# Convolution beside a feed-forward product: the second term of stage 1 summed in PSUM, the spectra multiplied in wider operations, and three row tiles taking turns

## The chip, the cores and the metric

The kernel runs on one core of a Trainium2 chip. The core has a matrix engine (TensorE, PE in the profile), VectorE (DVE), ScalarE (ACT), GpSimd (POOL) and SyncE (SP); each runs its own list of instructions in order, and semaphores tie the lists together. SBUF holds tiles of 128 partitions, and PSUM has eight banks of 128 x 512 float32 for the results of PE. DMA queues move data to and from DRAM. The metric is the device time of one execution in microseconds.

## What is computed

Two branches work on the layer-normalized input and are added to the input itself (2048 rows, 1024 channels, a hidden width of 3584):

```python
xn = layernorm(x)                                        # x = A_q, 1 x 2048 x 1024
k_shift = sum over 4 taps of shifted k * shift_k         # causal, per channel
kv = k_shift * v
y = irfft(rfft(kv, 4096) * rfft(ssm_k, 4096))[:2048]     # long causal convolution per channel
y = y + kv * ssm_D
conv = xn * y
ffn = silu(xn @ w1) @ w2                                 # 1024 -> 3584 -> 1024
return x + conv + ffn
```

Everything is float32. For the products in PE each operand is split into a float16 part `hi` and a float16 remainder `lo`, and each float32 product becomes three matmuls: hi by hi, hi by lo, lo by hi.

## The kernel before

*How the order of the work comes about.* No engine's list is written out by hand. Each part of the work is a Python generator (a stream) that yields operations: `T` for PE, `V` for DVE, `A` for ACT, `L` for a DMA issued by SP, `G` for a DMA issued by POOL that adds to what stands in DRAM (`accum_op=ADD`). `Order.run` takes, again and again, the operation that could start earliest by a model of engine times, less the bias of its stream; that puts it at the end of its engine's list. A stream can also yield a condition (a `Token`, or a free buffer) and is passed over until it holds. `Ring` is a set of named buffers; a tile that is taken from it is free again when its token has been set often enough. The bank rings of PSUM are `ff` (4 banks), `ps` (2), `px` (1) and `py` (1). Of the SBUF rings these matter here: `wo` (13 operand tiles, used for W1's factors and then for h), `v` (2), `hf` (3), `xg` (2), `yt` (2), `zh` and `zl` (2 each), `hi` and `lo` (2 each), `tmp` (1).

*The feed-forward branch* (`feed_forward`, from line 841). The first product runs per unit of hidden columns as seven block products P1 to P7 on sums and differences of blocks (`steps`, matmuls of 128 x 512 at lines 761 to 763); `evacuate` copies intermediate sums out of PSUM on ACT (into `v`, `w`) and adds them back on DVE (`hf<-ff,w`, `hf<-ff,v`); `block` applies SiLU, splits and writes h to DRAM. When that product is done, the second one runs: for each half `h` of 512 output columns and each of 16 row tiles `t`, one bank of `ff` collects 7 chunks `c` of 4 x 3 matmuls (lines 868 to 870), 84 in all, 2688 for the whole. `load_h` brings h's chunks on SP's queue in the order in which PE reads them. W2's chunks (`w2c[h, c]`) are split by `norms_w2` into places that the first product has left; the first row tile of a half is the first reader of each chunk. `result` scales a finished tile on ACT into a `v` buffer, and POOL adds it to the output. `copies` first writes x to the output (SP, line 918), one block of 128 rows after each half unit of the first product; no accumulating write may start before all sixteen copies are in the list (`flag["copied"]`).

*The convolution* (`convolution`). It goes over 8 groups `g` of 128 channels, beside the matrix products of the other branch, once the first part of the first product is over. For each group:
- `gate` makes `kv` and its energy; `norm` turns energies into powers of two as scales (a small matmul with ones, a DVE chain);
- `signal_parts`: for each of four `t` (in the order 1, 3, 0, 2) four transposes into `px` (line 1100) and splits into `hi`, `lo`;
- `stage1` (lines 1108 to 1134): a transform of length 128 as matmuls with the constants `cfw`. For each `t` and each half `c` (real, imaginary) two terms `i`, each of three matmuls of 128 x 512 into a bank of its own, from `ps` or, when the first product is over and more than one bank of `ff` is free (`spare`), from `ff`;
- `to_spec` (lines 1140 to 1150): with p0 and p1 the two banks, `total` = p0 (ACT copy), `diff` = total - p1, `total` = total + p1 (both DVE, reading PSUM);
- `forward`: the steps between the eight sub-transforms, on DVE;
- `product` (lines 1189 to 1227): the complex product of the two spectra, four pairs at a time, with `tmp`, a `zh` and a `zl` buffer as scratch; ACT squares the result for its energy, writing the squares to a `yt` buffer;
- `inverse`, `result_parts` (splits into `zh`, `zl`), `stage1_inv` (12 matmuls of 128 x 256 per `t` into `py`, lines 1331 to 1333), and `gated`: DVE multiplies `py` by the normalized rows `xg` into a `yt` buffer, and POOL adds that to the output in two writes (line 252), after which the buffer is free.

`stage1` of group g+1 starts when `product` of group g is over, since both use the spectrum `spec`. Four `gated` tiles per group and two `yt` buffers mean that the third and the fourth wait for the writes of the first and the second.

*Helpers whose lines appear in the profile:* line 248 is `L` (SP DMA), 252 `G` (POOL DMA), 255 `v_tt` (DVE, two tensors), 258 `v_stt` (DVE, scalar and two tensors), 266 `a_act` (ACT). Many parts share these lines, so they are told apart by the names of their tiles.

Of the kernel before, what the change touches and what calls it, by code (L numbers as in the profile page):

```python
# [12 lines left out]
BF16 = mybir.dt.bfloat16  # L13
F16 = mybir.dt.float16
# [198 lines left out]
def h3_ffn_kernel(ctx, tc, x, kp, vs, fs, shift, dskip, w1, w2, cfwd, cinv, out):  # L213
# [627 lines left out]
    def feed_forward():  # L841
# [12 lines left out]
        for h in range(2):  # L854
            for t in range(NT):
                yield ff.ready
                po, tok = ff.tile([P, W])
                final = (h, t) == (1, NT - 1)
                if final:
                    add(last_result(h, t, po, tok), EB)  # L860
                for c in range(NF // 4):
                    yield flag["h", h, t, c]
                    hx, htok = flag["h", h, t, c].what
                    yield flag["w2", h, c]
                    wc, wtok = w2c[h, c]
                    for jj in range(4):
                        def mm(jj=jj, j=4 * c + jj):
                            nc.tensor.matmul(po, hx[:, jj, 0, :], wc[:, jj, 0, :], start=(j == 0), stop=False)  # L868
                            nc.tensor.matmul(po, hx[:, jj, 0, :], wc[:, jj, 1, :], start=False, stop=False)  # L869
                            nc.tensor.matmul(po, hx[:, jj, 1, :], wc[:, jj, 0, :], start=False, stop=(j == NF - 1))  # L870
                        yield T(mm, po, [hx[:, jj], wc[:, jj]], 3 * 0.2185)
                    htok.set()
                    if t == NT - 1:
                        wtok.set()
                if final:
                    flag["last"].set()
                else:
                    add(result(h, t, po, tok), EB)
# [24 lines left out]
    def load_h():  # L903
        yield flag["factors"]
        for h in range(2):
            for t in range(NT):
                for c in range(NF // 4):
                    yield wo.ready
                    flag["h", h, t, c].what = o, _ = wo.tile([P, 4, 2, P], F16)
                    yield L(o, hs[t // 4][t % 4][:, 4 * c:4 * c + 4])  # L910
                    flag["h", h, t, c].set()
# [69 lines left out]
    def pair(a, b):  # L981
# [3 lines left out]
                       ap=[list(a.ap[0]), [b.offset - a.offset, 2]] + [list(d) for d in a.ap[1:]])  # L985

    TO = (1, 3, 0, 2)

    def convolution(floor):
# [118 lines left out]
        def stage1():  # L1108

            for g in range(NG):  # L1110
# [4 lines left out]
                for t in TO:  # L1115
                    yield flag["part", g, t]
                    (hi, htok), (lo, ltok) = part.pop((g, t))
                    for c in range(2):
# [343 lines left out]
```

## Time and profile before

| what | value |
| --- | --- |
| three runs | 1296.42, 1298.86, 1302.47 us |
| median | 1298.86 us |
| profiled execution, its own time | 1299.35 us |
| span of the profile in it | 1297.6 us |
| mean granted PE clock | 0.993 of full speed |

The page of the profile has one line per engine of how busy it is in 40 slices of the span, each slice 32.4 us long. A digit is the busy share in tenths (9 is 90% or more); PEclk is the granted clock in the same way:

```profile
PE   7899999999999998999999999999999999999998
DVE  8999997889999759999899899899899989989920
ACT  6867987887766856768523412512562252241120
POOL 0000000000000011001100200210110021011021
PEclk8999999999999998999999999999999999999999
```

PE is below nine tenths in the first two slices (layernorm and the first factors come before there is much to multiply), in the sixteenth (from 487 to 519 us) and in the last. In the rows below, a row of a timeline has the start in us, the duration in us, the engine, the line, the operation, out<-in tiles, sizes and types, and in brackets how long the engine stood before it and what ended that. A row of groups has the same for all instructions of one kind: count, busy us in sum, mean ns of one, then the idle time just before them and what ended most of it.

### The profile page before, as it was taken

To read this page: it belongs to the slowest core of one execution; us is meant where nothing else is said; L and a number is where in the kernel's file an instruction comes from. 1 tells how busy PE (TensorE), PEld (TensorE's weight loads), DVE (VectorE), ACT (ScalarE), POOL (GpSimd) and SP (SyncE) were. 2 spreads that over 40 slices of the span, in tenths; PEclk is the share of its full clock that TensorE was granted. 3 is DMA by queue.
4 is the path that set the end of the run, shared out by engine and by line. 5 is a ranking of instruction groups with operands and counts; after the bars stand their busy time and mean duration, and the time that the engine had idled before them with its cause. 6 is when DMAs were issued, how large, how long until landed. Compare 5 with 4: busy or idle time off the path is not lost.

```text
span 1297.6 us, 17976 instructions
## 1 busy us (share of the span) xinstructions
PE 1268.9 (98%) x6242; PEld 618.4 (48%) x6242; DVE 1145.9 (88%) x1758; ACT 691.9 (53%) x1238; POOL 98.4 (8%) x101
## 2 busy tenths in 40 slices
PE   7899999999999998999999999999999999999998
PEld 6444544444444543445444544544544454454453
DVE  8999997889999759999899899899899989989920
ACT  6867987887766856768523412512562252241120
POOL 0000000000000011001100200210110021011021
PEclk8999999999999998999999999999999999999999
DMA  9456899789998879869954664674596367456462
GB/s 324 163 163 211 291 318 311 255 263 348 323 324 284 273 214 285 262 207 296 294 168 100 148 186 136 151 191 129 137 290 190 97 156 190 111 112 133 114 138 33
DMA packets 207003, 269.93 MB, mean 208 GB/s; under 512 B 15416, under 2 KB 121920, under 8 KB 204480
## 3 DMA queue, kind: packets, MB, share of 16 engines
q1 hardware_dynamic: 185040, 252.26, 60.7%
q0 software_dynamic: 21872, 16.52, 10.3%
q8 instruction: 49, 0.80, 0.2%
q14 instruction: 42, 0.34, 0.1%
HBM read 193.22 MB, written 83.89 MB: 214 GB/s over the span
## 4 chain that ended last, share of the span: by engine, by line
PE 71%; DVE 17%; DMA 6%; issue 4%; ACT 2%; POOL 0%; SPq 0%; DVEq 0%; ACTq 0%; POOLq 0%
PE ff L763 12%; PE ff L761 12%; PE ff L762 12%; PE ff L869 9%; PE ff L870 9%; PE ff L868 9%; DVE spec L255 5%; DVE tmp L255 3%; DVE acc L258 2%; DMA out<-yt 2%; DMA kin<-in_kp 1%; DVE x L258 1%; PE ps L1127 1%; PE ps L1129 1%; PE ps L1128 1%
## 5 line engine op out<-in xcount | busy, mean ns | idle before, releaser
L869 PE MATMUL ff<-x,wo 128*128 128x512 f16 x896 | 340.7, 380 | 1.3 <-DVE x L258 1.3
L868 PE MATMUL ff<-x,wo 128*128 128x512 f16 x896 | 340.5, 380 | 0.8 <-ACT x L266 0.8
L870 PE MATMUL ff<-x,wo 128*128 128x512 f16 x896 | 340.5, 380 | 0.0
L761 PE MATMUL ff<-x,wo 128*128 128x512 f16 (+1 forms) x808 | 305.1, 378 | 5.7 <-ACT v L266 4.2
L762 PE MATMUL ff<-x,wo 128*128 128x512 f16 (+1 forms) x808 | 305.0, 377 | 2.1 <-DVE x L258 2.1
L763 PE MATMUL ff<-x,wo 128*128 128x512 f16 (+1 forms) x808 | 304.8, 377 | 2.1 <-DVE wo L258 2.1
L255 DVE TENSOR_TENSOR spec<-spec 128x512 f32<-128x512 f32 (+2 forms) x192 | 219.4, 1175 | 1.3
L870 PEld LDWEIGHTS <-wo 128*128 128x128 f16 x896 | 87.7, 98 | 107.7 <-issue 2.4
L868 PEld LDWEIGHTS <-wo 128*128 128x128 f16 x896 | 88.6, 99 | 101.1 <-issue 0.8
L869 PEld LDWEIGHTS <-wo 128*128 128x128 f16 x896 | 87.7, 98 | 102.2 <-issue 1.7
L252 POOL DMA_DIRECT2D out<-yt x64 | 70.5, 1102 | 810.2 <-DMA w2n<-in_w 430.9
L763 PEld LDWEIGHTS <-wo 128*128 128x128 f16 x808 | 79.4, 98 | 99.5 <-DVE wo L258 4.7
L762 PEld LDWEIGHTS <-wo 128*128 128x128 f16 x808 | 79.4, 98 | 92.4 <-issue 6.4
L761 PEld LDWEIGHTS <-wo 128*128 128x128 f16 x808 | 80.6, 100 | 88.5 <-ACT wo L266 2.1
L255 DVE TENSOR_TENSOR tmp<-spec 128x512 f32<-128x512 f32 (+1 forms) x112 | 100.3, 915 | 0.2
L258 DVE SCALAR_TENSOR_TENSOR ht<-hf,wsc,ht 128x512 f16<-128x512 f32 x112 | 83.4, 746 | 17.9 <-ACT ht L266 17.6
L266 ACT ACTIVATE ht<-hf,wsc 128x512 f16<-128x512 f32 x112 | 80.9, 722 | 3.6
L258 DVE SCALAR_TENSOR_TENSOR acc<-kin,taps,acc 128x512 f32<-128x512 f32 x96 | 71.7, 747 | 2.1 <-ACT acc L266 1.9
L266 ACT ACTIVATE xg<-xg,nmr,rstd 128x128 f32<-128x128 f32 x128 | 54.8, 482 | 34.9 <-DMA xg<-in_x 33.5
L266 ACT ACTIVATE zh<-spec,csc 128x1024 f16<-128x1024 f32 x32 | 36.1, 1142 | 66.4 <-DVE spec L258 49.1
L266 ACT ACTIVATE yt<-spec 128x1024 bf16<-128x1024 f32 x32 | 33.7, 1053 | 67.6 <-DVE spec L255 67.4
L266 ACT ACTIVATE v<-ff,invc 128x512 f32<-128x512 f32 x31 | 21.2, 683 | 89.5 <-PE ff L870 89.5
(151 smaller groups left out, 1756.2 us busy)
## 6 DMA issues: line engine op xcount, KB each, us to landing
wo<-hs SPq DMA_DIRECT2D x224, 256.0 KB, 3.0
hs<-ht SPq DMA_DIRECT2D x112, 256.0 KB, 4.6
ws<-wo SPq DMA_DIRECT2D x84, 256.0 KB, 3.6
wo<-ws SPq DMA_DIRECT2D x84, 256.0 KB, 3.7
w2n<-in_w SPq DMA_DIRECT2D x80, 256.0 KB, 4.7
raw<-in_w SPq DMA_DIRECT2D x28, 512.0 KB, 5.5
kin<-in_kp SPq DMA_DIRECT2D x32, 448.0 KB, 3.7
xt<-in_x SPq DMA_DIRECT2D x16, 512.0 KB, 7.2
```

Of the source, the lines that this page charges most:

```text
L252: return Op("POOL", 1.1, 4.0, lambda: nc.gpsimd.dma_start(o, i, accum_op=ADD), [i], [o], m, n)
L255: return V(lambda: nc.vector.tensor_tensor(o, a, b, op=op), o, [a, b], **k)
L258: return V(lambda: nc.vector.scalar_tensor_tensor(o, a, s, b, op0=op0, op1=op1), o, [a, b] + ([] if isinstance(s, float) else [s]), **k)
L266: nc.scalar.activation(o, i, func, scale=scale, **kw)
L761: nc.tensor.matmul(o, w[:, 0, k], xf[:, :, k, 0], start=first and k == 0, stop=False, **kw)
L762: nc.tensor.matmul(o, w[:, 0, k], xf[:, :, k, 1], start=False, stop=False, **kw)
L763: nc.tensor.matmul(o, w[:, 1, k], xf[:, :, k, 0], start=False, stop=last and k == KH - 1, **kw)
L868: nc.tensor.matmul(po, hx[:, jj, 0, :], wc[:, jj, 0, :], start=(j == 0), stop=False)
L869: nc.tensor.matmul(po, hx[:, jj, 0, :], wc[:, jj, 1, :], start=False, stop=False)
L870: nc.tensor.matmul(po, hx[:, jj, 1, :], wc[:, jj, 0, :], start=False, stop=(j == NF - 1))
L1127: nc.tensor.matmul(ps, cf[:, 0, cs], hi[:, i], start=True, stop=False)
L1128: nc.tensor.matmul(ps, cf[:, 0, cs], lo[:, i], start=False, stop=False)
```

## The change

Four things are edited.

1. *Stage 1.* The two terms of a pair now use one bank. The first term's three matmuls write it (for both `c`), ACT copies it to `diff` (times 2), and then the second term's matmuls accumulate upon it in the same bank; they wait for the copy (`seen`). ACT then copies the sum to `total`, and DVE takes one difference: 2 p0 - (p0 + p1) = p0 - p1. The loops over `i` and `c` change places, so that the first terms of both `c` come ahead of the second ones.
2. *Product.* The products of the spectra are taken in operations of 2048, 1024 and 512 elements, through access patterns written out by `steps_of` and `run`, partly in place in the second spectrum; `zh` and `zl` are no longer used for it, nor a `yt` buffer for the squares, which go into a part of the spectrum that is no longer needed. With that `transforms` no longer waits for `more`, the rings that come late.
3. *Second matrix product.* In the first half, the row tiles 0, 1 and 2 take turns: chunk `c` is multiplied for all three before chunk `c + 1`, with three banks open at once (`TOGETHER`). All other row tiles go one by one, as before. `load_h` follows the same order.
4. *What follows from it for the lists.* The scheduler lays all lists out anew with these costs and conditions. The number of matmuls is the same.

```diff
         flag["gemm1"].set()
         for h in range(2):
-            for t in range(NT):
-                yield ff.ready
-                po, tok = ff.tile([P, W])
-                final = (h, t) == (1, NT - 1)
-                if final:
-                    add(last_result(h, t, po, tok), EB)
+            for ts in TOGETHER[h]:
+                pos = {}
                 for c in range(NF // 4):
-                    yield flag["h", h, t, c]
-                    hx, htok = flag["h", h, t, c].what
-                    yield flag["w2", h, c]
-                    wc, wtok = w2c[h, c]
-                    for jj in range(4):
-                        def mm(jj=jj, j=4 * c + jj):
-                            nc.tensor.matmul(po, hx[:, jj, 0, :], wc[:, jj, 0, :], start=(j == 0), stop=False)
-                            nc.tensor.matmul(po, hx[:, jj, 0, :], wc[:, jj, 1, :], start=False, stop=False)
-                            nc.tensor.matmul(po, hx[:, jj, 1, :], wc[:, jj, 0, :], start=False, stop=(j == NF - 1))
-                        yield T(mm, po, [hx[:, jj], wc[:, jj]], 3 * 0.2185)
-                    htok.set()
-                    if t == NT - 1:
-                        wtok.set()
-                if final:
-                    flag["last"].set()
-                else:
-                    add(result(h, t, po, tok), EB)
+                    for t in ts:
+                        final = (h, t) == (1, NT - 1)
+                        if c == 0:
+                            yield ff.ready
+                            pos[t] = ff.tile([P, W])
+                            if final:
+                                add(last_result(h, t, *pos[t]), EB)
+                        yield flag["h", h, t, c]
+                        hx, htok = flag["h", h, t, c].what
+                        yield flag["w2", h, c]
+                        wc, wtok = w2c[h, c]
+                        for jj in range(4):
+                            def mm(jj=jj, j=4 * c + jj, po=pos[t][0]):
+                                nc.tensor.matmul(po, hx[:, jj, 0, :], wc[:, jj, 0, :], start=(j == 0), stop=False)
+                                nc.tensor.matmul(po, hx[:, jj, 0, :], wc[:, jj, 1, :], start=False, stop=False)
+                                nc.tensor.matmul(po, hx[:, jj, 1, :], wc[:, jj, 0, :], start=False, stop=(j == NF - 1))
+                            yield T(mm, pos[t][0], [hx[:, jj], wc[:, jj]], 3 * 0.2185)
+                        htok.set()
+                        if t == NT - 1:
+                            wtok.set()
+                        if c == NF // 4 - 1:
+                            if final:
+                                flag["last"].set()
+                            else:
+                                add(result(h, t, *pos[t]), EB)
+    TOGETHER = ([range(3)] + [(t,) for t in range(3, NT)],
+                [(t,) for t in range(NT)])
...
-            for t in range(NT):
-                for c in range(NF // 4):
-                    yield wo.ready
-                    flag["h", h, t, c].what = o, _ = wo.tile([P, 4, 2, P], F16)
-                    yield L(o, hs[t // 4][t % 4][:, 4 * c:4 * c + 4])
-                    flag["h", h, t, c].set()
+            for c, t in [(c, t) for ts in TOGETHER[h] for c in range(NF // 4) for t in ts]:
+                yield wo.ready
+                flag["h", h, t, c].what = o, _ = wo.tile([P, 4, 2, P], F16)
+                yield L(o, hs[t // 4][t % 4][:, 4 * c:4 * c + 4])
+                flag["h", h, t, c].set()
...
+    def steps_of(a, start, *dims):
+        return run(a, start, 1, *dims)
+    def run(a, start, n, *dims):
+        return bass.AP(tensor=a.tensor, offset=a.offset + start,
+                       ap=[list(a.ap[0])] + [list(d) for d in dims] + [[1, n * P]])
...
                 for t in TO:
                     yield flag["part", g, t]
                     (hi, htok), (lo, ltok) = part.pop((g, t))
-                    for c in range(2):
-                        cs = slice(c * P, (c + 1) * P)
-                        two = []
-                        for i in range(2):
-                            yield lambda: ps_r.ready() or spare()
-                            ps, tok = (ps_r if ps_r.ready() else ff).tile([P, 2, 2 * P])
-                            cf = cfw[:, t + 4 * i]
+                    two = []
+                    for i in range(2):
+                        for c in range(2):
+                            if i == 0:
+                                yield lambda: ps_r.ready() or spare()
+                                ps, tok = (ps_r if ps_r.ready() else ff).tile([P, 2, 2 * P])
+                                two.append((ps, Token(), Token(), Token()))
+                                diff = (tmp[:, :, t // 2] if t % 2 else sp[:, :, 5 + t])[:, :, c]
+                                add(to_spec(g, t, sp[:, :, t, c, :], diff, *two[c], tok), CB)
+                            ps, seen, made = two[c][:3]
+                            if i == 1:
+                                yield seen
 
                             def mm():
-                                nc.tensor.matmul(ps, cf[:, 0, cs], hi[:, i], start=True, stop=False)
-                                nc.tensor.matmul(ps, cf[:, 0, cs], lo[:, i], start=False, stop=False)
-                                nc.tensor.matmul(ps, cf[:, 1, cs], hi[:, i], start=False, stop=True)
+                                cf = cfw[:, t + 4 * i, :, c * P:(c + 1) * P]
+                                kw = dict(skip_group_check=i == 1)
+                                nc.tensor.matmul(ps, cf[:, 0], hi[:, i], start=i == 0, stop=False, **kw)
+                                nc.tensor.matmul(ps, cf[:, 0], lo[:, i], start=False, stop=False, **kw)
+                                nc.tensor.matmul(ps, cf[:, 1], hi[:, i], start=False, stop=True, **kw)
                             yield T(mm, ps, [hi[:, i], lo[:, i]], 0.65, m=2.0)
-                            two += [ps, tok]
-                        diff = (tmp[:, :, t // 2] if t % 2 else sp[:, :, 5 + t])[:, :, c]
-                        add(to_spec(g, t, sp[:, :, t, c, :], diff, *two), CB)
+                            (made if i else two[c][3]).set()
                     htok.set()
                     ltok.set()
 
         def spare():
             return flag["gemm1"]() and len(ff.free()) > 1
 
-        def to_spec(g, t, total, diff, p0, tok0, p1, tok1):
+        def to_spec(g, t, total, diff, ps, seen, made, half, tok):
+            yield half
             if g > 0:
                 yield flag["taken", g - 1, t]
                 if t % 2 == 0:
                     yield flag["taken", g - 1, t + 1]
-            yield a_act(total, p0, AF.Copy)
-            tok0.set()
-            yield v_tt(diff, total, p1, SUB)
-            yield v_tt(total, total, p1, ADD)
-            tok1.set()
+            yield a_act(diff, ps, AF.Copy, 2.0)
+            seen.set()
+            yield made
+            yield a_act(total, ps, AF.Copy)
+            yield v_tt(diff, diff, ps, SUB)
+            tok.set()
             flag["spec", g, t % 2].set()
 
...
             yield tmp_r.ready
-            tmp, tok = tmp_r.tile([P, 2, 2, 2, 2 * P])
-            t1, t2 = tmp[:, 0], tmp[:, 1]
-            yield more["zh"].ready
-            o1, k1 = more["zh"].tile([P, 4, P])
-            yield more["zl"].ready
-            o2, k2 = more["zl"].tile([P, 4, P])
-            a1 = t1.rearrange("p s c (q w) -> p (s c) q w", q=2)
-            a2 = t2.rearrange("p s c (q w) -> p (s c) q w", q=2)
+            tmp, tok = tmp_r.tile([P, 2, 2, 4, P])
             flag["energy", g].n = 4
             for n in range(4):
                 xx, k = sp[:, 0, 2 * n:2 * n + 2], sp[:, 1, 2 * n:2 * n + 2]
-                xf = xx.rearrange("p s c w -> p (s c) w")
-                kk = k.rearrange("p s c w -> p (s c) w")
-                yield v_tt(a1, xf[:, :, None, lo].to_broadcast([P, 4, 2, P]),
-                           kk.rearrange("p m (q w) -> p m q w", q=2), MUL)
-                yield v_tt(o1, xf[:, :, hi], kk[:, :, lo], MUL)
-                for c in range(2):
-                    yield v_tt(a2[:, c::2], xx[:, :, c, None, lo].to_broadcast([P, 2, 2, P]),
-                               k[:, :, 1 - c].rearrange("p s (q w) -> p s q w", q=2), MUL)
-                yield v_tt(o2.rearrange("p (s c) w -> p s c w", c=2), xx[:, :, :, hi],
-                           pair(k[:, :, 1, lo], k[:, :, 0, lo]).rearrange("p c s w -> p s c w"), MUL)
-                yield v_tt(a1[:, :, 1], a1[:, :, 1], o1, ADD)
-                yield v_tt(a2[:, :, 1], a2[:, :, 1], o2, ADD)
-                yield v_tt(xx[:, :, 0], t1[:, :, 0], t1[:, :, 1], SUB)
-                yield v_tt(xx[:, :, 1], t2[:, :, 0], t2[:, :, 1], ADD)
-                add(energy(g, xx.rearrange("p s c w -> p s (c w)"), ss[:, 8 + n:9 + n]), CB)
+                yield v_tt(run(tmp, 0, 16), steps_of(xx, 0, (2 * P, 4), (0, 4)), run(k, 0, 4, (4 * P, 2), (0, 2)), MUL)
+                for s in range(2):
+                    yield v_tt(steps_of(k, (4 * s + 3) * P, (-P, 2), (-2 * P, 2)),
+                               steps_of(xx, (4 * s + 3) * P, (0, 2), (-2 * P, 2)),
+                               steps_of(k, (4 * s + 2) * P, (-2 * P, 2), (0, 2)), MUL)
+                o = steps_of(tmp, P, (2 * P, 8))
+                yield v_tt(o, o, run(k, 0, 8), ADD)
+                t = tmp.rearrange("p s c (d w) v -> p s c d (w v)", d=2)
+                yield v_tt(xx[:, :, 0], t[:, :, 0, 0], t[:, :, 1, 1], SUB)
+                yield v_tt(xx[:, :, 1], t[:, :, 0, 1], t[:, :, 1, 0], ADD)
+                add(energy(g, xx.rearrange("p s c w -> p (s c w)"), sp[:, 1, 2 * n + 1].rearrange("p c w -> p (c w)"),
+                           ss[:, 8 + n:9 + n]), CB)
             tok.set()
-            k1.set()
-            k2.set()
             flag["product", g].set()
 
-        def energy(g, o, s):
-            yield more["yt"].ready
-            j, tok = more["yt"].tile([P, 2, 4 * P], BF16)
-            yield a_act(j, o, AF.Square, 2.0 ** -48, total=s)
-            tok.set()
+        def energy(g, o, j, s):
+            yield a_act(j.bitcast(BF16), o, AF.Square, 2.0 ** -48, total=s)
             flag["energy", g].set()
 
...
                 yield from forward(g)
-                yield lambda: bool(more)
                 yield from product(g)
```

## The prediction, made before the changed kernel had run

> **What bounds the kernel now.** I read the page's busy shares and chain first, then busy time by stretch, then what TensorE (PE) waits for, then the timeline around each of those waits.
>
> ```profile
> span 1297.6 us, 17976 instructions
> PE 1268.9 (98%) x6242; PEld 618.4 (48%) x6242; DVE 1145.9 (88%) x1758; ACT 691.9 (53%) x1238; POOL 98.4 (8%) x101
> PE 71%; DVE 17%; DMA 6%; issue 4%; ACT 2%; POOL 0%; SPq 0%; DVEq 0%; ACTq 0%; POOLq 0%
> 450.00:500.00 50.00, 45.80 (x206) 20.59 (x204) 35.28 (x41) 30.54 (x65) 7.71 (x7) 0.93 0.86 239
> 950.00:1000.00 50.00, 47.88 (x214) 21.17 (x213) 49.81 (x59) 19.49 (x34) 4.87 (x5) 0.97 0.85 266
> 1000.00:1250.00 250.00, 250.00 (x1248) 122.62 (x1246) 226.96 (x306) 76.91 (x135) 31.38 (x31) 1.00 0.56 132
> 1250.00:1298.00 48.00, 43.62 (x209) 20.13 (x206) 1.50 (x2) 1.53 (x3) 7.28 (x7) 1.00 0.36 64
> ```
>
> The stretches give stretch, length, then busy time of PE, weight loads, VectorE (DVE), ScalarE (ACT) and POOL, the granted clock, and DMA. From 1000 to 1250 us PE never stops, and in the last 48 us DVE works for 1.50 us: the convolution is over and PE alone finishes the second matrix product. The kernel ends when PE has done its list, so an edit counts only as it adds or removes PE waiting. Two stretches above hold such waits, and their granted clock is lower too, 0.93 and 0.97. DVE at 88% looks near a bound, but it isn't what ends last.
>
> ```profile
> 478.79 0.38 PE L761 MATMUL ff<-x,wo 128*128 128x512 f16 x1
> ...
> 488.93 0.38 PE L763 MATMUL ff<-x,wo 128*128 128x512 f16 x1
> 493.51 0.58 PE L761 MATMUL ff<-x,wo 128*128 128x512 f16 x1 [4.20 <-ACT v L266]
> 493.89 0.63 PE L762 MATMUL ff<-x,wo 128*128 128x512 f16 x1
> ...
> 499.01 0.59 PE L762 MATMUL ff<-x,wo 128*128 128x512 f16 x1
> 499.44 0.38 PE L763 MATMUL ff<-x,wo 128*128 128x512 f16 x1
> ```
>
> From 478.79 to 488.93 lie 47 starts: 10.14 / 47 = 0.2157 us each, PE's pace, which is my unit for time between two places in PE's order. Then comes the longest wait of the steady part. After it 12 starts take 5.12 us (493.89 to 499.01), 0.427 each: PE runs at half pace until 499.44. From 488.93 to 499.44 pass 10.51 us for 15 starts that need 3.24: the wait costs 7.3 us, not 4.2.
>
> **The cause of that wait** matters, for the change moves it:
>
> ```profile
> 461.21 0.56 SPq L918 DMA_DIRECT2D out<-in_x  x1
> 468.55 1.11 POOL L252 DMA_DIRECT2D out<-yt  x1 [35.05 <-DMA out<-in_x]
> 476.64 1.11 POOL L252 DMA_DIRECT2D out<-yt  x1 [2.60 <-issue]
> 476.38 0.68 DVE L255 TENSOR_TENSOR hf<-ff,w 128x512 f32<-128x512 f32 x1
> 483.85 0.75 DVE L258 SCALAR_TENSOR_TENSOR yt<-py,csc,xg 128x512 f32<-128x512 f32 x1 [5.66 <-DMA wo<-ws]
> 489.24 0.69 DVE L255 TENSOR_TENSOR hf<-ff,v 128x512 f32<-128x512 f32 x1
> 492.88 0.58 ACT L266 ACTIVATE v<-ff 128x512 f32<-128x512 f32 x1
> ```
>
> The last copy of x to out is issued at 461.21; POOL's accumulating writes of gated rows queue behind it (468.55, and the fourth at 476.64). The fourth gated row of group 0 reuses a yt buffer that this fourth write must have left, so DVE stands 5.66 us until 483.85. (The row names another DMA; the buffer fits the instruction's own waits.) DVE's next sum for the first product, 489.24, is late, ACT behind it copies v at 492.88, and PE goes on at 493.51.
>
> **The change part by part**, against the profiled execution's 1299.35 us (0.04% over the median of the three runs, 1298.86; 1.75 us of it outside the span).
>
> *Stage 1.* PE's matmuls are the same in number. DVE loses one of its two sums per pair, ACT gains a copy:
>
> ```profile
> L255 DVE TENSOR_TENSOR spec<-spec,ps 128x512 f32<-128x512 f32 x73 | 49.9, 684 | 9.1 <-PE ps L1129 7.1 <-ACT spec L266 1.1
> L266 ACT ACTIVATE spec<-ps 128x512 f32<-128x512 f32 x45 | 26.2, 583 | 11.4 <-PE ps L1129 6.3 <-DVE zl L258 5.1
> ACT acc L266 <- DMA kin<-in_kp: 43.7, 18, 5.0
> ```
>
> There are 64 pairs (8 groups, 4 t, 2 c): DVE 64 x 0.684 = 44 us less, ACT 64 x 0.583 = 37 us more, some 729 of 1298. DVE's gain lies beside PE's matrix products, so it counts 0; were DVE the bound, it would be -44. New is a wait: the second term's matmuls wait for ACT's first copy. In the changed instruction order 15 to 130 matmuls stand between the halves (in the shortest windows some are of 256 columns, counted half), so at least 15 x 0.2157 = 3.2 us for a copy of 0.58. What queues behind the waiting matmul is all of PE. What can delay ACT is a DMA wait ahead of the copy (up to 5.0 us in the row above). If ACT is never more than 3.2 - 0.58 = 2.6 us late the price is 0; if in each of eight groups one such DMA wait meets a shortest window, 8 x (5.0 - 2.6) = 19. I take +1, nearer the low end, because the order before also put bank releases by ACT in front of stage-1 matmuls and the waits of the whole trace show none of PE for them.
>
> *Product.* Nine operations of 1024 and 8 x 512 elements become six of 2048, 1024 and 4 x 512, the same elements:
>
> ```profile
> L255 DVE TENSOR_TENSOR spec<-spec 128x2048 f32<-128x2048 f32 x24 | 54.9, 2287 | 0.4
> L255 DVE TENSOR_TENSOR tmp<-spec 128x1024 f32<-128x1024 f32 x48 | 58.3, 1221 | 0.2
> L255 DVE TENSOR_TENSOR zh<-spec 128x512 f32<-128x512 f32 x32 | 22.0, 686 | 0.0
> ```
>
> By these means 6.71 us become 6.25, 32 times: at most 15 us less on DVE. The new order has sums directly behind what they read, which takes part of it back, so 0 to 15; off PE's path, 0. The squares now use dead halves of the spectrum in place of yt, and the product no longer holds zh and zl: no path, 0.
>
> *Row tiles in turns.* Each chunk of W2 serves three tiles before the next is needed.
>
> ```profile
> 626.90 0.75 DVE L258 SCALAR_TENSOR_TENSOR x<-w2n,tau,x 128x512 f16<-128x512 f32 x1
> 630.29 0.38 PE L869 MATMUL ff<-x,wo 128*128 128x512 f16 x1
> ```
>
> The last split of the first half's seventh chunk ends at 627.65, 2.6 us before the matmul that reads it: there is no wait to remove. Three banks held at once leave no spare bank for stage 1 in that time, which the order already shows, and there stage 1 keeps its place: 0. SP issues the same loads of h, in the order in which PE reads them: 0. The three results now come out together, so the third ACT copy waits for POOL's first write (5.8 us at group 1's rate below), but the fourth tile has the fourth bank and PE needs the third's only a tile later, 84 x 0.2157 = 18 us: 0.
>
> *Writes at group 0.* In SP's order the last two copies now stand one transfer earlier, ahead of a spill of h. But in DVE's order the blocked gated row now stands ahead of the sum hf<-ff,w (which ran at 476.38, before the block), with one operation of 1.1 us between. PE needs that sum at 478.79. If the write lands when it did, PE waits until 483.85 + 0.7 + 1.1 + 0.7 = 486.4, 7.6 us in place of 4.4: +3. If the copies' 2 to 4 us earlier issue passes through, 4 to 6 us: 0. If the write lands by 477, the wait and its slow stretch go: -7.3. I take +1.
>
> *Writes at group 1.* POOL's writes run one after the other:
>
> ```profile
> 584.32 0.75 DVE L258 SCALAR_TENSOR_TENSOR yt<-py,csc,xg 128x512 f32<-128x512 f32 x1
> 585.48 1.09 POOL L252 DMA_DIRECT2D out<-yt  x1 [87.23 <-DVE yt L258]
> 608.69 1.09 POOL L252 DMA_DIRECT2D out<-yt  x1 [5.81 <-DVE ht L258]
> 714.90 1.11 POOL L252 DMA_DIRECT2D out<-yt  x1 [2.50 <-DVE yt L258]
> 733.47 1.11 POOL L252 DMA_DIRECT2D out<-yt  x1 [2.76 <-issue]
> 733.33 0.75 DVE L258 SCALAR_TENSOR_TENSOR yt<-py,csc,xg 128x512 f32<-128x512 f32 x1 [4.77 <-DMA out<-yt]
> ```
>
> Four writes take 23.2 us at group 1 (585.48 to 608.69), 18.6 at group 2 (714.90 to 733.47), where the fourth gated row stood 4.77 us for them. At group 1 PE's order had 72 matmuls of 512 and 36 of 256 columns from the first inverse block to the fourth (90 full ones, 19.4 us); now 48 and 36 (66, 14.2). So here too the fourth gated row comes before its buffer is free. Directly behind it stands the DVE difference that frees a bank for stage 1. PE reaches that matmul 22.7 us after the first inverse block (87 matmuls of 512 columns and 36 of 256); the difference is done 1.2 + 18.6 to 23.2 + 0.75 + 0.7 = 21.2 to 25.8 us after it. PE waits 0 to 3.1 us, with half pace behind it 0 to 6. I take +3. From group 2 on nothing that PE needs soon stands behind the fourth row: 0.
>
> *Sum:* 1299.35 + 1 + 1 + 3 = 1304 us.
>
> How a wait is priced bears on this. Half pace also followed short waits:
>
> ```profile
> 975.23 0.38 PE L869 MATMUL ff<-x,wo 128*128 128x512 f16 x1 [0.63 <-DVE x L258]
> 977.69 0.58 PE L869 MATMUL ff<-x,wo 128*128 128x512 f16 x1 [0.66 <-DVE x L258]
> 980.63 0.42 PE L870 MATMUL ff<-x,wo 128*128 128x512 f16 x1
> 783.72 0.63 PE L1100 MATMUL px<-ident,acc 128*128 128x128 f32 x4 [1.04 <-DVE pow L360]
> 790.57 0.66 PE L1100 MATMUL px<-ident,acc 128*128 128x128 f32 x4 [1.04 <-DVE lo L258]
> ```
>
> From 977.69 to 980.63, 7 starts take 0.42 each after waits below 1 us, while the two lone ones of 1.04 lost no more than their length. The Trainium skill (TensorE: Matmul & The Clock Gate, Part 1: The HAM clock gate) says that the clock halves after an idle window of about 3.4 us; by that rule a wait under it costs only itself, and half of 3.1 would stand for group 1, and the sum would be an estimate of 1303. The rows at 975 us speak against it, so I keep half of a slow stretch in the term for group 1.
>
> **The rivals.**
> - *Faster, 1290 us:* the copies' earlier issue frees group 0 in time (-7.3) and DVE's lighter list ends the two lone waits for px (-2). For it: the earlier SP place, 44 us less on DVE. Against: the sum now stands behind the blocked row.
> - *Both write queues bind, 1310 us:* +3 at group 0, +6 at group 1, +1. For it: 23.2 us of writes against 14.2 of PE. Against: a lighter DMA load would shorten the writes.
> - *Slower, the accumulating half waits for ACT, 1322 us:* one shortest window overrun in each of eight groups, 19 us, beside the writes' +4. It decides when ACT is more than 2.6 us late at the first copy. For it: 37 us more on ACT, DMA waits up to 5.0. Against: 3.2 us or more for 0.58.
> - *The change does nothing for the end:* DVE's 44 us turn into idle time. That is inside the forecast.
>
> **How the numbers follow.** I call within 0.5% (1292.4 to 1305.3) no change, about what a measurement of this kernel can tell. Forecast around 1304: 0.50, of which 0.45 within and 0.05 above; faster case 0.17; both write queues 0.19; ACT case 0.14. Faster 0.17, same 0.45, slower 0.38. The forecast's own range is 1298 to 1309. The range is 1290 to 1316: it takes in half of the faster case and all of the write case and cuts off most of the ACT case, some 0.2 in all.
>
> **What would show it.** The first half's difference gone from DVE's groups (64 fewer reads of PSUM), 64 more ACT copies, DVE near 1095 us, PE's busy matmuls unchanged. At 479 us a PE wait of 4 to 8 us on the c bank (by DVE hf) in place of 4.2 on ACT v, with half pace behind it; near 590 to 600 us a wait of PE ps on DVE spec. No wait of PE ps on ACT beyond 1 us elsewhere. The forecast is wrong if PE has no wait near 479, or if stage-1 matmuls wait on ACT in group after group.

## The result, and the profile after

| kernel | median us | lowest to highest | runs |
| --- | --- | --- | --- |
| before | 1300.03 | 1296.42 to 1302.47 | 12 |
| changed | 1304.20 | 1300.07 to 1306.67 | 12 |

The ratio is 1.0031, with a 95% interval of 1.0017 to 1.0044: about 4 us slower, where 1304 was forecast. Now the page of the changed kernel, its span, its busy times and its chain:

```profile
span 1304.9 us, 17805 instructions
PE 1270.4 (97%) x6242; PEld 619.7 (47%) x6242; DVE 1106.9 (85%) x1598; ACT 723.5 (55%) x1302; POOL 98.4 (8%) x101
PE 78%; DVE 10%; DMA 6%; issue 4%; ACT 2%; POOL 0%; SPq 0%; DVEq 0%; ACTq 0%; POOLq 0%
```

PE has the same 6242 matmuls and the same busy time to 1.5 us. DVE is 39.0 us lighter with 160 operations fewer (64 in stage 1, 3 in each of 32 products), ACT 31.6 us heavier with 64 more. None of DVE's 39 us shows at the end.

The two profiled executions can't be compared by their ends alone. The lists of all engines agree up to some 282 us of the kernel before, and there the changed kernel is already 5.0 us behind. Timelines of PE, before and after, at the same instruction:

```profile
250.95 0.38 PE L763 MATMUL ff<-x,wo 128*128 128x512 f16 x1
```

```profile
255.98 0.38 PE L763 MATMUL ff<-x,wo 128*128 128x512 f16 x1
```

That is how far two executions of the same instructions differ. To place the rest I took, for each pair of neighbouring matmuls, the distance of their starts beyond the pace of 0.2157 us (0.109 for 256 columns), and added it up by stretch, from 242 us on. The stretches hold group 0's gated rows (440 to 530 us), group 1's (530 to 622), the first readers of W2 in the first half (622 to 665), and the seam of the two halves (940 to 1010):

| kernel | 440-530 | 530-622 | 622-665 | 665-940 | 940-1010 | all from 242 on |
| --- | --- | --- | --- | --- | --- | --- |
| before | 7.3 | 0.1 | 0 | 3.2 | 4.1 | 14.9 |
| changed | 9.1 | 2.3 | 0 | 2.3 | 3.4 | 17.6 |

The change adds 1.8 us at group 0 and 2.2 us at group 1 and takes 1.6 away later: +2.7 in this pair of executions. Group 0 in the changed kernel's timelines (start, duration, engine, line, operation; in brackets the wait):

```profile
434.65 1.25 POOL L252 DMA_DIRECT2D out<-yt  x1 [433.35 <-ACT zh L266]
473.56 1.11 POOL L252 DMA_DIRECT2D out<-yt  x1 [37.66 <-DMA w2n<-in_w]
478.52 0.75 DVE L258 SCALAR_TENSOR_TENSOR yt<-py,csc,xg 128x512 f32<-128x512 f32 x1 [4.30 <-issue]
479.32 0.28 PE L1342 MATMUL py<-zh,civ 128*128 128x256 f16 x1 [2.48 <-DVE yt L258]
482.47 1.11 POOL L252 DMA_DIRECT2D out<-yt  x1 [2.68 <-issue]
486.25 0.38 PE L763 MATMUL ff<-x,wo 128*128 128x512 f16 x1
488.72 0.75 DVE L258 SCALAR_TENSOR_TENSOR yt<-py,csc,xg 128x512 f32<-128x512 f32 x1 [5.39 <-issue]
490.52 0.68 DVE L255 TENSOR_TENSOR hf<-ff,w 128x512 f32<-128x512 f32 x1
491.26 0.48 PE L761 MATMUL ff<-x,wo 128*128 128x512 f16 x1 [4.63 <-DVE hf L255]
491.53 0.63 PE L762 MATMUL ff<-x,wo 128*128 128x512 f16 x1
494.51 0.53 PE L763 MATMUL ff<-x,wo 128*128 128x512 f16 x1
```

Less the 5.03 us of the start, POOL's second write goes out at 468.53, against 468.55 before: the earlier place of the copies came to nothing. The fourth gated row then starts at 488.72 - 5.03 = 483.69 (483.85 before), the sum `hf<-ff,w` behind it ends late, and PE goes on at 486.23, where the prediction had 486.4. A wait of 2.48 us for the third gated row is new as well: until that row has read `py`, PE can't write the next inverse block there. Group 1:

```profile
602.30 0.75 DVE L258 SCALAR_TENSOR_TENSOR yt<-py,csc,xg 128x512 f32<-128x512 f32 x1 [2.48 <-DMA w2n<-in_w]
603.70 0.38 PE L1150 MATMUL ps<-hi,cfw 128*128 128x512 f16 x1 [0.25 <-DVE spec L255]
611.01 0.38 PE L761 MATMUL ff<-x,wo 128*128 128x512 f16 x1 [0.67 <-ACT v L266]
615.13 0.38 PE L761 MATMUL ff<-x,wo 128*128 128x512 f16 x1 [0.73 <-ACT w L266]
```

The fourth gated row waits again, the bank of stage 1 behind it costs 0.25 us, and two copies on ACT are late after it.

### The profile page after: what moved, and what is told of

It reads as the page before. It is cut to its first block, busy times and chain, and to the rows that moved or that the text cites. A ratio compares the mean times of both kernels' runs of the same rounds, so it can differ in the third digit from the quotient of the medians.

```text
span 1304.9 us, 17805 instructions
## 1 busy us (share of the span) xinstructions
PE 1270.4 (97%) x6242; PEld 619.7 (47%) x6242; DVE 1106.9 (85%) x1598; ACT 723.5 (55%) x1302; POOL 98.4 (8%) x101
## 4 chain that ended last, share of the span: by engine, by line
PE 78%; DVE 10%; DMA 6%; issue 4%; ACT 2%; POOL 0%; SPq 0%; DVEq 0%; ACTq 0%; POOLq 0%
PE ff L872 12%; PE ff L873 12%; PE ff L871 12%; PE ff L763 11%; PE ff L762 11%; PE ff L761 11%; DVE spec L255 3%; PE ps L1150 2%; PE ps L1152 1%; PE ps L1151 1%; DVE x L258 1%; DVE tmp L255 1%; DMA raw<-in_w 1%; PE px L1116 1%; DMA w2n<-in_w 1%
## 5 line engine op out<-in xcount | busy, mean ns | idle before, releaser
L255 DVE TENSOR_TENSOR spec<-spec 128x512 f32<-128x512 f32 (+2 forms) x256 | 260.9, 1051 | 2.0
L255 DVE TENSOR_TENSOR tmp<-spec 128x2048 f32<-128x2048 f32 (+1 forms) x48 | 92.4, 1932 | 0.8
L266 ACT ACTIVATE spec<-spec 128x1024 bf16<-128x1024 f32 x32 | 33.7, 1054 | 65.5 <-DVE spec L255 65.4
```

Of the source, the lines that this page charges most:

```text
L255: return V(lambda: nc.vector.tensor_tensor(o, a, b, op=op), o, [a, b], **k)
L266: nc.scalar.activation(o, i, func, scale=scale, **kw)
```

## The experiments

The first four ask whether the writes are the cause, and what stage 1's edit does by itself.

**Writes of groups 0 and 1 left out**, in both kernels; all other lists stay as they are:

```diff
-                yield G(out4[b][:, :, t, g * P:(g + 1) * P], yt[:, b])
+                p = G(out4[b][:, :, t, g * P:(g + 1) * P], yt[:, b])
+                if g < 2:
+                    p.emit = lambda: None
+                yield p
```

> The kernel before, with POOL's accumulating writes of groups 0 and 1 of the convolution left out and every other engine's list as it was (those rows of the output lack the convolution). Write-queue theory: the PE wait near 489 us with its half pace goes, 7.3 us, so 1300.0 - 7.3 = 1293 us. Rival (the wait has another cause, ACT or a load of operands): within 2 us of 1300.

> The changed kernel, with the same writes of groups 0 and 1 left out and its other lists kept (those rows of the output lack the convolution). Write-queue theory: the waits near 479 and 491 us (9 us with half pace) and the slow stretch from 603 to 615 us (2 us) go, so 1304.2 - 11 = 1293 us, and no more than 2 us are left between this and the kernel before without the same writes. Rival (the change costs its 4 us elsewhere, by waits of the accumulating half for ACT or in the row tiles that take turns): it stays 4 us above the kernel before without the writes.

Measured: 1292.80 us, ratio to before 0.9941 (95% interval 0.9926 to 0.9956, and so in brackets from here on), and 1292.57 us, 0.9945 (0.9931 to 0.9959). The write-queue theory had 1293 for both. Busy time by stretch (stretch, length, then busy time of PE, weight loads, DVE, ACT, POOL, the clock, DMA), of the changed kernel and of the one without the writes:

```profile
440.00:500.00 60.00, 52.90 (x251) 24.86 (x250) 37.45 (x44) 38.82 (x83) 6.60 (x6) 0.97 0.81 233
565.00:625.00 60.00, 58.35 (x297) 29.09 (x296) 47.40 (x70) 49.90 (x84) 8.79 (x8) 1.00 0.91 253
```

```profile
440.00:500.00 60.00, 60.00 (x294) 28.62 (x293) 47.13 (x54) 47.33 (x101) 0.00 (x0) 1.00 0.86 268
565.00:625.00 60.00, 59.96 (x306) 29.96 (x305) 46.02 (x64) 51.59 (x92) 0.00 (x0) 1.00 0.82 261
```

Without the writes PE stands for 0.04 us in these stretches, and the two kernels are level: their ratios differ by 0.0004, and each has an interval of 0.003. So the writes are the cause of both stalls, and with them gone no difference that these runs could tell is left between the kernels; DVE's 39 us are worth nothing clear of that either.

**Copies earlier**, `yield flag["unit", a // 4]` in place of `a // 2` in `copies`, in the changed kernel. The copies had been issued two after each of eight half units; now four go after each of the first four:

> The changed kernel, with the sixteen copies of x to the output issued in the first four half units of the second half of the first product instead of eight (four copies each). Write-queue theory: the last copy lands before the first gated row of group 0 is there, so the block at group 0 goes: about 9 us less, 1295 us, and PE doesn't wait between 470 and 500 us. Rival (the copies only move their load onto the transfers of operands and of h): new PE waits between 330 and 420 us, 1304 us or more.

Measured: 1294.42 us, 0.9960 (0.9946 to 0.9974). This run's stretches and POOL's writes:

```profile
440.00:500.00 60.00, 60.00 (x294) 28.60 (x293) 46.10 (x55) 48.09 (x103) 6.61 (x6) 1.00 0.93 262
565.00:625.00 60.00, 57.50 (x288) 28.67 (x287) 49.05 (x74) 50.26 (x90) 8.79 (x8) 0.97 0.97 276
```

```profile
433.52 1.25 POOL L252 DMA_DIRECT2D out<-yt  x1 [432.21 <-DMA hs<-ht]
438.59 1.11 POOL L252 DMA_DIRECT2D out<-yt  x1 [3.83 <-issue]
```

The second write goes out 5 us after the first, not 39, and group 0's stall is gone. What was late was the last copies' place in the list: the change moved them by one transfer, and here they are moved by four half units. Group 1 stays (4.4 us). No run moved its writes, so whether their place in the queue or their load on the DMA queues holds it is not told apart.

**Stage 1 alone**, on the kernel before:

> The kernel before with the edit of stage 1 alone (second term accumulated, one difference). Write-queue theory: DVE loses 44 us and the end loses nothing; the block at group 0 stays at 7 to 9 us: 1299 to 1303 us. Rival (the accumulating half waits for ACT): waits of PE for ACT at stage 1 in group after group, up to 19 us: 1310 us or more. Rival (DVE was a bound): 1290 us or less.

Measured: 1312.48 us, 1.0094 (1.0076 to 1.0112). That is dearer by 12 us, yet not by waits for ACT at the accumulating half: the excess is 11.6 us at group 0, 2.4 at group 1, and 7.9 at a place where the kernel before loses nothing:

```profile
640.67 0.38 PE L869 MATMUL ff<-x,wo 128*128 128x512 f16 x1 [0.91 <-DVE x L258]
642.44 0.38 PE L868 MATMUL ff<-x,wo 128*128 128x512 f16 x1 [1.18 <-ACT x L266]
644.26 0.38 PE L869 MATMUL ff<-x,wo 128*128 128x512 f16 x1 [1.45 <-DVE x L258]
647.38 0.58 PE L869 MATMUL ff<-x,wo 128*128 128x512 f16 x1 [0.90 <-DVE x L258]
```

Here the first row tile waits for the splits of W2's seventh chunk, which had 2.6 us to spare before. That is above the range of the write-queue theory, and in the number the rival's case, without its cause: no stage-1 matmul waits for ACT in this trace. I had costed the turns of row tiles at nothing, because there was no wait to remove. The new theory ("cover theory" below) was that the turns give W2's splits the time that the other two edits take from them.

**The turns taken out, and each of the other parts alone.** The kernels are the changed one without `TOGETHER`, the one before with `TOGETHER` only, and the one before with the new product only.

> The changed kernel with the row tiles of the second product one by one again (stage 1 and product as changed). Cover theory (stage 1's edit makes the first row tile wait for W2's chunks, as its alone-run showed near 640 us with 7.3 us of PE lost, and the turns give each chunk three times as long): waits for W2's splits near 620 to 650 us are back, 1304.2 + 5 to 8 = 1309 to 1312 us. Rival (the turns do nothing, the product's shorter list healed it): 1304 us with no such wait.

> The kernel before with the turns of three row tiles alone. Cover theory: there the first tile had no wait for W2 to be removed, so the turns give nothing, 1300 us, at most 3 us more if they draw the inverse blocks of group 1 together. Rival (the turns help by themselves): 1297 us or less. Rival (the turns cost the 4 us, by banks held): 1304 us with waits of PE for banks.

> The kernel before with the edit of the product alone. DVE is not what ends last, so its 0 to 15 us of shorter work give nothing: 1298 to 1302 us, with the block at group 0 near 489 us as before. Rival (a list laid out anew brings its own waits, as the stage-1 edit alone showed): 1303 us or more, with a wait at another place than 470 to 500 us.

Without the turns: 1308.47 us, 1.0066 (1.0048 to 1.0085), just under the range of the cover theory, and the wait is back:

```profile
632.92 0.38 PE L868 MATMUL ff<-x,wo 128*128 128x512 f16 x1 [0.30 <-ACT x L266]
635.56 0.38 PE L869 MATMUL ff<-x,wo 128*128 128x512 f16 x1 [2.26 <-DVE x L258]
638.02 0.58 PE L869 MATMUL ff<-x,wo 128*128 128x512 f16 x1 [1.26 <-DVE x L258]
```

In the changed kernel the last split of that chunk starts 26.6 us ahead of the matmul that reads it:

```profile
644.75 0.74 DVE L258 SCALAR_TENSOR_TENSOR x<-w2n,tau,x 128x512 f16<-128x512 f32 x1
```

```profile
671.39 0.38 PE L872 MATMUL ff<-x,wo 128*128 128x512 f16 x1
```

The turns alone: 1294.43 us, 0.9965 (0.9951 to 0.9980), a gain, as the first rival had it. All lists agree with those of the kernel before until h's second chunk is loaded at 569 us, so group 0's smaller loss in this execution (4.8 us against 7.3) is the spread of the same instructions. What the turns changed lies behind that: between 665 and 940 us PE loses 0.7 us in place of 3.2 (the two waits of 1.04 us for `px`, at 783 and 790 us before, are gone from the newly laid lists), and at the seam of the halves nothing in place of 4.1. Busy times of the stretch 970 to 980 us before, then with the turns alone:

```profile
970.00:980.00 10.00, 7.88 (x31) 3.08 (x30) 10.00 (x14) 4.25 (x6) 0.00 (x0) 0.86 0.82 309
```

```profile
970.00:980.00 10.00, 10.00 (x48) 4.50 (x47) 10.00 (x12) 2.13 (x4) 1.96 (x3) 1.00 0.87 202
```

The seam's window runs from the last reader of W2's first chunk in the first half, which frees a place, to the first reader of the seventh chunk in the second. In six of the eight combinations of the three edits no matmul of the convolution stands in it, and these lose 2.0 to 6.3 us at the seam (table below). In the two with the turns and without stage 1's edit some do, and these lose 0 and 0.5: 73 with the product's edit, and with the turns alone a block of 21, 9 of stage 1 and 12 of the inverse. The first and the last of those 9, and of the 12:

```profile
938.39 0.38 PE L1134 MATMUL ps<-hi,cfw 128*128 128x512 f16 x1
941.41 0.38 PE L1136 MATMUL ff<-hi,cfw 128*128 128x512 f16 x1
943.57 0.27 PE L1338 MATMUL py<-zh,civ 128*128 128x256 f16 x1
944.77 0.27 PE L1340 MATMUL py<-zh,civ 128*128 128x256 f16 x1
```

They take 9 x 0.2157 + 12 x 0.109 = 3.2 us, by which the splits have more time; the last one ends 3.6 us before it is needed. So this part of the gain comes from where the convolution's blocks happen to fall. That the place of that block decides is read from the traces; no run moved it alone.

The product alone: 1308.36 us, 1.0067 (1.0051 to 1.0084), as its rival had it: lists laid out anew bring their own waits. DVE's busy time in it is 1144.2 us, 1.7 less than before, at the low end of 0 to 15. Its loss is 9.3 us at group 0, 5.8 between 665 and 940 and 6.3 at the seam, for instance:

```profile
896.31 0.63 PE L1109 MATMUL px<-ident,acc 128*128 128x128 f32 x4 [0.52 <-DVE pow L360]
903.80 0.66 PE L1109 MATMUL px<-ident,acc 128*128 128x128 f32 x4 [1.04 <-DVE lo L258]
986.87 0.38 PE L869 MATMUL ff<-x,wo 128*128 128x512 f16 x1 [2.54 <-DVE x L258]
```

**The two missing pairs**, stage 1 with the turns, and the product with the turns:

> The changed kernel with the product as before (stage 1 and the turns of row tiles kept). Cover theory (the turns take away the wait for W2's chunks that stage 1's edit brings): 1312.5 - 7.3 = 1305 us, no wait for W2 between 620 and 660 us, the block at group 0 as in the changed kernel (about 9 us). Rival (the turns only gave what they gave alone, 5.6 us by luck of the later list): the W2 wait stays near 640 us.

> The changed kernel with stage 1 as before (product and turns kept). If stage 1's edit is what costs the changed kernel its 4 us (its gated rows now stand ahead of the sums that PE needs): 1300 us or less, with the block at group 0 as in the kernel before (5 to 8 us). If the product's edit costs as much in any list, as alone: 1304 us or more.

Measured: 1303.73 us, 1.0040 (1.0024 to 1.0056), and 1302.15 us, 1.0026 (1.0013 to 1.0039). The first is as the cover theory had it, with no wait for W2 near 640 us. The second lies between its two cases and decides for neither. All eight combinations, with the loss of PE by stretch in each one's profiled execution:

| stage 1 | product | turns | ratio | 440-530 | 530-622 | 622-665 | 665-940 | 940-1010 |
| --- | --- | --- | --- | --- | --- | --- | --- | --- |
| - | - | - | 1 | 7.3 | 0.1 | 0 | 3.2 | 4.1 |
| x | - | - | 1.0094 | 11.6 | 2.4 | 7.9 | 0.7 | 2.0 |
| - | x | - | 1.0067 | 9.3 | 1.5 | 0.1 | 5.8 | 6.3 |
| - | - | x | 0.9965 | 4.8 | 0.5 | 0.5 | 0.7 | 0 |
| x | x | - | 1.0066 | 8.3 | 2.1 | 7.4 | 0.2 | 2.1 |
| x | - | x | 1.0040 | 10.3 | 2.6 | 0 | 0.2 | 2.5 |
| - | x | x | 1.0026 | 7.4 | 2.3 | 0.2 | 5.4 | 0.5 |
| x | x | x | 1.0031 | 9.1 | 2.3 | 0 | 2.3 | 3.4 |

Each row is one execution, and the same instructions spread by 2.5 us at group 0. With stage 1's edit group 0 loses 8.3 to 11.6 us, without it 4.8 to 9.3; without the turns it opens the wait for W2, and with them that wait is gone. Between 665 and 1010 us the kernels with it lose less than the kernel before (2.3 to 5.7 against 7.3), though the turns alone lose only 0.7 there. Since this edit is what takes 40 us off DVE, the question was what those are worth once group 0 and W2 are out of the way.

**Both covers at once.** Early copies, and three tiles in turns in the second half too (`TOGETHER` with `[range(3)]` in both lists), on the changed kernel and then on the kernel before (with the turns in the first half added):

> The changed kernel with the early copies and with the first three row tiles taking turns in the second half of the columns too. If the waits for W2's splits near 971 to 977 us (4.6 us lost with early copies) go the way they went in the first half, 1294.4 - 4 = 1290 us. Rival (the raw W2 loads are late there by more than three tiles cover, or three open banks take stage 1's spare bank): 1294 us or more, with waits near 960 to 980 us or of stage 1 for banks.

> The kernel before (stage 1 and product as they were) with early copies and with three tiles in turns in both halves. If DVE's 39 us less busy time are worth nothing at the end, taking away the block at group 0 (5 to 7 us) and the W2 waits of the second half (4 us) gives 1300 - 10 = 1290 us, level with the 1291.0 of the changed kernel with the same two edits. Rival (with the waits gone DVE's shorter list counts): 1294 us or more, 3 us above it.

Measured: 1291.04 us, 0.9939 (0.9922 to 0.9956), and 1297.07 us, 0.9989 (0.9974 to 1.0004). The first beats both kernels: its loss from 242 us on is 6.3 us, its seam has no wait for W2. The second stays 6 us above it, which is the rival's number but not its cause: 3.9 of its loss lie between 440 and 530 us, where stage 1 waits 3.1 us for a bank that DVE has not left, and DVE is not busy there but stands:

```profile
453.98 0.75 DVE L258 SCALAR_TENSOR_TENSOR yt<-py,csc,xg 128x512 f32<-128x512 f32 x1 [6.97 <-DMA wo<-ws]
456.10 0.38 PE L1134 MATMUL ps<-hi,cfw 128*128 128x512 f16 x1 [3.06 <-DVE spec L255]
```

It is the fourth gated row of group 0 again, whose buffer POOL's fourth write (issued at 448.00) must leave, and the differences that free the bank stand right behind it. With stage 1's edit that row comes at 466.61 and doesn't wait. So in this pair the writes still hold PE, and it doesn't price DVE's length. For that, **DVE's work was put back without moving anything**:

```diff
-            yield v_tt(diff, diff, ps, SUB)
+            p = v_tt(diff, diff, ps, SUB)
+            sub = p.emit
+            p.emit = lambda: (sub(), nc.vector.tensor_tensor(diff, diff, diff, op=ALU.max))
+            yield p
```

> The changed kernel with early copies and turns in both halves (1291.0 us), and in stage 1 a second operation of 512 elements on DVE after each difference (the maximum of the difference with itself), which puts the 64 operations and some 40 us back on DVE while every list keeps its order. If DVE's length is what separates the two kernels once the writes and W2 no longer hold PE: 1294 to 1297 us, with waits of PE for DVE at the transposes of px or at gated rows. If it was only the order of the lists: 1291 to 1292 us.

Measured: 1299.21 us, 1.0010 (0.9999 to 1.0021), 8 us above the same lists without the 64 operations (9 by the two ratios), and above the 1294 to 1297 expected. The pages of the two, the lighter first, and the longest waits that are new or longer in the second:

```profile
PE 1267.4 (98%) x6242; PEld 619.5 (48%) x6242; DVE 1105.7 (86%) x1598; ACT 724.1 (56%) x1302; POOL 98.4 (8%) x101
```

```profile
PE 1268.0 (98%) x6242; PEld 619.1 (48%) x6242; DVE 1147.2 (88%) x1662; ACT 722.1 (56%) x1302; POOL 98.5 (8%) x101
```

```profile
349.38 0.38 PE L761 MATMUL ff<-x,wo 128*128 128x512 f16 x1 [1.59 <-ACT v L266]
509.24 0.38 PE L761 MATMUL ff<-x,wo 128*128 128x512 f16 x1 [2.22 <-ACT ff L266]
611.29 0.38 PE L761 MATMUL ff<-x,wo 128*128 128x512 f16 x1 [2.51 <-ACT w L266]
```

41.5 us of DVE make 8 us of time. They lie where the first product's sums and copies come late, and not, as was expected, at `px` or the gated rows; the scheduler had not planned for the added operations, so this prices 41.5 us in lists that were laid out without them. With the writes left out and lists laid out for each, 39 us were worth nothing. So these runs have shown 0 us and 8 us for some 40 us of DVE, and what it is worth for another list stays open.

## Why the prediction was right, and where its steps were not

- *Group 0, +1 of -7.3 to +3:* the right mechanism, and the case that came is the one at +3. The write landed when it did before, PE went on at 486.23 against 486.4 forecast, and the new order cost +1.8 us in the profiles (more against the 4.8 us that the same lists as before showed in another execution). The wait of 2.48 us for the third gated row was in no case. The middle case, that the copies' earlier issue passes through, didn't happen at all.
- *Group 1, +3 of 0 to 6:* right cause, since the loss goes with the writes, and 2.2 us, but by another path: the stage-1 bank that the prediction watched cost 0.25 us, and the rest came at late copies of `v` and `w` in the first product. That the size still fits the term is luck.
- *Accumulating half, +1 of 0 to 19:* no such wait in the changed kernel. The order leaves little, though: two pairs of matmuls started 0.05 us after the copy they wait for.
- *Turns at 0, "there is no wait to remove":* the step that failed. It was true of the list before, and wrong as a price: stage 1's edit made a wait of 7 us there, and the turns hid it. Going from two edits to three is worth 1308.47 - 1304.20 = 4.3 us.
- *Product at 0:* failed by itself (+8.4 us alone). Its gain on DVE was 1.7 us, and the re-laid lists lost at group 0, at `px` and at the seam.
- *DVE's 44 us at 0, since PE ends last:* held in the pair without writes, whose lists were planned for it, and not as a rule: put into finished lists 41.5 us cost 8. DVE's busy time is 1106.9 us where the prediction looked for about 1095. An engine that isn't last still sets when PE's banks come free, as at 603.70 us.
- *The sum:* 1304 against 1304.2. Its two terms of writes are where the profiles differ, and without the writes the kernels are level, so it was right for its reason. That it meets the median to 0.2 us is luck: single terms had ranges of 6 to 19 us, and in the profiles they came out at 1.8, 2.2 and 0 with 1.6 taken away later. And taken alone the parts of the change made some +12 us (stage 1), +8 (product, set to nothing) and -5 (turns, set to nothing), and only together come to +4: the working doesn't show why they cancel.
- *How a wait is priced:* the 2.48 us wait at 479.32 was followed by matmuls of 256 columns at their pace (0.109 us apart), and only the 4.63 us one by eight starts of 0.43. That agrees with the rule of the Trainium skill (TensorE: Matmul & The Clock Gate, Part 1: The HAM clock gate) that the clock halves after an idle window of about 3.4 us. The rows without the turns show that the window need not be idle throughout: after waits of 2.26 and 1.26 us the starts from 638.02 to 641.44 are 0.43 apart on average. Stretch by stretch (busy times as above, the granted clock the third number from the end):

```profile
632.43:635.84 3.41, 0.85 (x4) 0.25 (x3) 3.41 (x4) 1.89 (x3) 0.00 (x0) 1.00 0.92 333
635.84:642.67 6.83, 5.57 (x14) 1.69 (x13) 6.83 (x10) 3.16 (x6) 0.00 (x0) 0.50 0.50 155
```

In each of the fourteen traces the granted clock changes only at whole multiples of 3.41 us from its other changes, so time falls into windows of that length. From 242 to 1280 us, each of eleven windows at full clock in which PE stood for 73% or more (here 75%) was followed by half clock, two of nine with 50 to 58% were, and none with less. The lone wait of 2.48 us took 27% of one window and 46% of the next. So what a wait of 2 to 5 us costs hangs on how it falls upon these windows, and a bound from one wait alone is too low.

## What to carry to other kernels

An edit that removes no wait may still be the cover that other edits of the same change use up: where several edits draw on the same slack (2.6 us here), price them together, and say for each cover what it costs when it is gone. When a long queue serves a late starter (writes that wait for the last of sixteen copies), first move the late starter: that took 0.7% off the changed kernel (0.9960 against 1.0031), where one transfer's place gave nothing. And compare profiles from the last instruction up to which the lists agree.

## What the runs showed of the hardware

Two executions of the same instructions differed by 5.0 us in their first 256 us and by 2.5 us in the stall of group 0 (7.3 and 4.8); a single profile could not have told these kernels apart. The 2.5 us go with the clock: in the kernel before, the stall filled 96% of one window of 3.41 us and half clock followed, while with the turns alone it fell upon two windows, 52 and 43% of them, and the clock stayed full. POOL's accumulating writes don't start closer together when the copies no longer compete: in the changed kernel no two of group 0 are less than 3.7 us apart (492.53 and 496.19), with the copies early no two less than 4.4 (455.47 and 459.85).
